# New orders, engine choices and PSUM banks for a four-layer attention kernel

## The chip, the core and the metric

The kernel runs on one core of one Trainium2 chip. The metric is the device time of one execution in microseconds (us), as the median of several runs. The engines are PE (TensorE; its weight loads are listed apart, as PEld), DVE (VectorE), ACT (ScalarE), POOL (GpSimd) and SP (SyncE, which only issues DMAs here).

## The reference

Four layers with residual sums act on x of 2048 tokens by 512 features, in bf16. Layers 1 and 3 are linear attention with 32 heads of 16, layers 2 and 4 softmax attention in a window of 256 keys:

```python
x = x + _A_ref(_layernorm(x), A_wqkv, A_wo)   # phi(q) (phi(k)^T v) / (phi(q) sum phi(k)), then @ wo
x = x + _B_ref(_layernorm(x), B_wqkv, B_wo)   # softmax over keys with 0 <= i - j < 256, then @ wo
x = x + _A_ref(_layernorm(x), A_wqkv, A_wo)
x = x + _B_ref(_layernorm(x), B_wqkv, B_wo)
# phi(t) = where(t > 0, t + 1, exp(t)) + 1e-6
```

## The kernel before, in words

The tokens are cut into 16 tiles of 128. x (`xres`), all weights and the keys and values of four tiles stay in SBUF. PSUM is used as eight banks of 128 x 512 fp32 (one bank is a tile of the plan).

The program is written as a graph of 2559 operations (`Graph.add`, class `Op`). An operation is one thing that one engine does: a group of matmuls, an eviction from PSUM, a mask, a DMA. It knows what it reads and writes and which PSUM tiles it uses. The names that the prediction and the experiments use are these:

- `norm` (the line numbers are the profile's): statistics (L374, DVE), their aggregate (L375, DVE), variance plus epsilon (L379, POOL; L377 on DVE for a few), the power -1/2 (L380, POOL), the subtraction and scaling (L381, DVE), and a transpose by DMA (L389, SP) or for a few tiles by PE (L395) with an eviction (L402).
- `tok` (L420) and `feat` (L434): the projections on PE, token-major and feature-major. L501 to L524 are the sums over keys of layer 1, L480 and L477 those of layer 3 and their normalizers.
- `phi`: the exponential (L444, ACT), minimum (L447, DVE), and the maximum (L451, DVE, or L446 on ACT and L449 on DVE).
- Plain evictions (L407): `bqe` of queries and `bve` of values of the softmax layers, `ve` of the values of layer 3, `ge`, `Me` and `sc` in the passages between layers. `bke` (L627 on ACT, L628 on DVE) evicts keys into a spread layout. Each of these may be ACT's or DVE's.
- `s` (L676, L712, L745, L792): scores of one tile of keys, in parts; `ex` (L686, L721, L754, L801): their exponentials on ACT; `mk` and `md` (L694, L726): causal masks on DVE; `mf`: the masks of the far keys, on POOL (L772) or DVE (L773). `pv` (L822): products with the values; `rcp` and `div` (L834, L835); `oT`: the transposed output; `bout` (L420): the output projection; `res` (L604): the residual sum on DVE. `outp` (L942): the store of one tile of the result, from SP or POOL; the very last tile is stored in two halves (L878, after L877).
- `fill`: seven matmuls on zeros that PE runs at the start, beside nine before them.

Layer 1 computes all keys first; then a passage with PE's L501 to L579 follows; layer 2 then goes tile by tile, interleaved with the norms and keys of layer 3. After a second passage (layer 3's queries, sums and normalizers) comes layer 4, with the output projection of layer 3 interleaved tile by tile.

What sets the order: one table, `TABLE`, a compressed string. `place(g)` (L92) unpacks it. It holds, for 2559 operations, the overall order (two bytes each), the engine of each operation (one byte each), and the bank of each of 1005 PSUM tiles (one byte each). Each engine issues its operations in that order, and no other. A PSUM tile waits for all users of the tile that held its bank before. For a few pairs `place` adds a wait: a long POOL operation (`LONG`) waits for the short DVE operation (`SHORT`) that stands last ahead of it in the order. `synchronise` then turns dependences into semaphore waits.

```python
order = [ops[raw[2 * k] + 256 * raw[2 * k + 1]] for k in range(n)]
o.eng = ("PE", "ACT", "DVE", "POOL", "SP")[raw[2 * n + o.i]]
x.banks = [raw[3 * n + k]]
```

The planner's keys and costs in `PAR` don't count here, since the table overrides them.

Of the kernel before, what the change touches and what calls it, by code (L numbers as in the profile page):

```python
# [235 lines left out]
class Plan:  # L236
# [718 lines left out]
    r"c-qZZ1GH_+j;*AUO4YS(+qP}nwr$(CZQHhO+h*^z&%Lkz@5lf8{~o>0SxP0TnVDHN_6n(#3ZYPu0>vt{(khG!tBeY#;;UdPxccG}D67J&gzBTqtRkpSE~5J8",  # L955
    r"5~(cegG;Qksun7VilmaNY^tS-tg@?Cs*n2YqNp6IwMwQYsGKUfimLi5QE62hl|uDX(NtR%N~Ke|RXdeZEmn<GdevXmRuk0{HA!Vqb<_a0O)XUeRbACyrBahs",
    r"V>L)^R~^(cHAU4^JJeJaL)BLuRT{NZEmtvBF_lrRP@U9ZwM)fPomF&oOYK&%RYR3Y4N<q%3Ds5IQA1TX6;}mT2I8o@s=Lag;;Cuso@$~}tCMP&y050IH|msX",
    r"sv4-_YKA(kR;rn5l{%y5s#)r+TCEDIE=r(>daH`7HEN#9t0F*8wMPX~7J8`>s)SmrMk)ur)hP8&1%ml1BJ5SURA4BhvcMd*PmNZIV1b&g_N(_QE38usRV4VJ",
    r"&Zz_HqlygYRdrPi8o&khKqZDKkOYduLv>L_g>2AFtyh=SBb84bRF72<$PQ0bP$&VHRSpOSC84>>2~X7+6&yaPr0`jdQ)5*rIHbO)WY7?j!&emzzNxAzI$Tj9",
    r"pftpQ{OXyC2?}CC1(ge&8n1Fg5S0Q7sXUMp@<J#`1^J+`Dg$L9HGEfPRT>xvjUXhHgE$aW6;S0N9aMnvPyi}H5!D!KLu_aYwP2A-3sqEps0c+>JE#FQVS}ou",  # L960
    r"+Cv?v3-zF!st+BY2^?0Pp@wP$9iauZg;vlKHmWYr3|hkx)d`wIcX+Ojs;{mGOn|O%OihI2YLlw0UZ_d1SzT2x)k4^!CPO8)2(GCq&<&=-3D~L@!*$gYrol;=",
    r"4mZ>$SOV45W>^X{;1mEXgPCwsAuNZvumUvnf_bnKN~&2<Ud@Lsa2RT-*{}e%!V#DQ+n_g`hNG|@*1{{*57xnP*a0_TJ?w;4&<A$GYUm5MU=5rBf{?fYUaPZk",
    r"8%kqMbqxB$J=h4Lkl_K8!E+EAOR3OsAI`%wD2o>$47`BdP!9J%SO|l6VIMq)aBv6q!(NDm2Ounlhqn+8W8*srj~Ah|ii4NnJw(8`_y{h;6?g&%p*&uNhfo0{",
    r";sAII*B~)g#DQ=gli~$D1eLH3Cc%qX8RO$qsEY}3EY`ytFb)&q2e=NYaXfy6PmmVlVS4xs8K6FXfi!pttKdtxjIUq<W`rx49wT7}oQSXCDrSPnI0=(sReS>(",
    r"aWY21sE8O16Ja&X3=OdXCdcU52&>~YOo5GY3bw^eI2CJPI&6<AaUQ0^`B)R%p~mY-xB#0XV`glQ9WV<Te1OgHD+p%AhiEYyeurt82Opus>G%zrU`GsuG4Te@",
    r"z|MFR17i!U47acoDy#y4*)cEH#vGUrYhg>wiTSY=7Qh%-6&7O`j0;OKH_pUrFbiAb608onFbEdJpx6eN;c_g5!EiR-#+7&ngJWTg2SqRhuE3($74Kp<j1Q}D",
    r"J$A<guo@TPMob86um^6yemDr$;yN4*n{gp-#i39Pi{lX3f)VvFh@>}R34Dp$@HLji?N|zT;46%*zhV?!O@G7cdMEC}{`ehh=mYo^qv`=zQ$NROx*!b1Cs+ug",
    r">t`54_ryUMQzz1e;RVjtz3>gr(SxxFJkYgtQK+qZV`BXnhu~cOP$$ttu@8R4gZK%D;URpahhtwH4xjNb?nb5O;#=H<BcP7HkMD3Ve!)4ITG!R@5%dvEtM?=7",
    r"4_Hs9(T{a<y$@sQCtB;2I<_W#4@Y1e{Zt3iDfCE8r=RJ}dY&GIjdW6-MaR{naSX=OS@nE<6tnA8`WQCW@pTTJUN_Olae>aDbLxe<jb5ZP>iW8^&ZHaY6PQc4",
    r"(<iZmey#)SY`UTDsDtQaI=61GgX&J2bsil|8{J$7*Ligd-C2jwqVwq<x}`3nd+9aW>QmTLC(urx#>KjiK7(s@Kix&I(;;<h-BtJ1p>!*K7B}i{`W%MVn{`p$",  # L970
    r"T^G~+^(Nh0Z`H;10G&{8(<Ssky<L~o`SliEN)OV@byGc97tkwoY28dO(Pi{Xy+Ie$d-YPiUw_nv^)g*nf71K(NC=}x>QV4nht;DYoIa>u=&_KL4(ntTUXOu7",
    r"x|}|w*XsznyiQIP^bkEt57ia*OI=C7(!+EL8m)KellrwzNn>;?N=2u1YdWG+(@uRrpVnz;mmaRu(pZf&Lch^OZD_TAt9R?8dX*lhHMOPj`k3CM-{}eZtp29c",
    r"(Q&P4qFzrY^dx;oZ=mlw5N)LNbWR5*pp2A(GEop>`l5r;CNlIvhoGP&)Q;Zk%+#KOQ*QdI&+87<k@C_7ZE3Q06q54L6n#-=qwF+QU()%h6HU{h=&~+A)Abb{",
    r"nsU%pU64vs7|KasC@htwuT+R4Q$FfOW$2pjPTwdO6{o^fj!M#Xy_tGY5!yl}XaH@cqSTp+(LgFiUFbWNr$MB+D-EFvG?cc{4PB9L>S0ugYEU>jK(}-h3QxCn",
    r"RJx;kQv`}eS*Q;kr0BGr`cg!iK!<3Co<uWs49ZH8C??gUi8Poh(=1(!Vo_BBj!nC1IK`noRGW~i&=}G@g6a_QI2uWNX)GP3$<&W_P+b~D_2?M&r=2vOM$=tg",
    r"pL)`9x~CgZFN#aMs5;%(4XGNPq$zZYrqXG;N{4A0ouGI$ovzanvh4U81?50Imx6J8x<MD|3^k(56r3AV0y;~VC?TDrCUk{D@p-yQO(`^Apk{Q7!f-ea$+u}9",
    r"-J$S2pO_a=1b#%(I4m1pNYObbhu~bih=gPCVrovgc?K<^7POyc(qn2#`{)VHqL>_upHd=<&57w5wdFXxl<razT1K;}9p9%p^qgOC5WYtzxIG8vlN^y>aw3kz",
    r"uQ&<E<>wTcU-Jt}%**K%zoZrPfTD0zF2pM-9v9(N6rW$wYD&t5IUncc1iXe4@@vY^YbhB&q>H?cPICdy!=?BVC+9MJhA;CKF3knG92e!Qe3mP4F}}vdxjc8{",
# [190 lines left out]
```

## Time and profile before

| | |
|---|---|
| median of 3 runs | 412.56 us (412.19 to 414.08) |
| span of the profiled execution, first to last instruction | 410.8 us |
| granted TensorE clock | 1.000 |
| DMA, mean | 91 GB/s |
| operations by the table: PE, ACT, DVE, POOL, SP | 866, 447, 806, 212, 228 |

The profiled execution has no other time than its span; the median of the runs is 1.8 us above it, for what lies around the first and the last instruction. The profile page gives busy times by engine, the chain of work that ended last (followed back from the last instruction, at each step to what released it), and groups of instructions by line. In a row such as "L694 DVE TENSOR_TENSOR pb<-pb,tri 128x512 ...", the tile written stands left of the arrow, and those read right of it.

### The profile page before, as it was taken

What the parts mean: (1) busy time and instruction counts of PE and PEld (TensorE: products, weight loads), DVE (VectorE), ACT (ScalarE), POOL (GpSimd) and SP (SyncE); (2) the same over time, 40 slices, a digit from 0 to 9 for tenths busy, and PEclk for the clock granted to TensorE, in tenths of its full rate; (3) what the DMA queues carried; (4) which work ended last, traced back from release to release, by engine and by line L of the source; (5) the groups of instructions that cost most, each with busy time, mean ns of one, the idle gap of its engine ahead of it and who ended that gap; (6) DMA issues with size and microseconds to landing.
All of it is one profiled execution on the core that took longest, in us unless ns stands there. A gap on an engine that the chain in (4) does not pass through costs nothing.

```text
span 410.8 us, 17540 instructions
## 1 busy us (share of the span) xinstructions
PE 386.9 (94%) x7668; PEld 260.3 (63%) x7742; DVE 344.5 (84%) x807; ACT 352.8 (86%) x448; POOL 122.4 (30%) x216
## 2 busy tenths in 40 slices
PE   7999999999999999999999999999999988999896
PEld 3654676766575576566567777586757755566674
DVE  6997799989998899888887789997899688857585
ACT  4654659998999999999998357999999999999993
POOL 4576653111252331320503203303113304303020
PEclk9999999999999999999999999999999999999999
DMA  7495114443243435353222100344314821561751
GB/s 249 101 217 144 49 34 115 120 70 90 56 106 74 119 77 107 81 119 82 68 41 57 27 2 2 105 109 81 102 44 122 122 66 41 120 127 56 168 107 42
DMA packets 66596, 37.19 MB, mean 91 GB/s; under 512 B 47640, under 2 KB 61848, under 8 KB 66520
## 3 DMA queue, kind: packets, MB, share of 16 engines
q1 hardware_dynamic: 66032, 34.75, 37.0%
q8 instruction: 61, 1.00, 1.1%
q0 software_dynamic: 480, 1.31, 1.0%
q14 instruction: 15, 0.12, 0.1%
q10 hardware_dynamic: 8, 0.00, 0.0%
HBM read 6.29 MB, written 2.10 MB: 20 GB/s over the span
## 4 chain that ended last, share of the span: by engine, by line
PE 51%; ACT 34%; DVE 9%; DMA 3%; issue 2%; SPq 1%; POOL 1%
ACT pb L686 20%; PE ps L420 18%; PE ps L434 10%; PE ps L822 10%; PE ps L676 5%; ACT pb L801 5%; ACT vp L686 4%; PE ps L501 3%; ACT tE L444 2%; DMA wA<-in_A_wqkv_dram 2%; DMA xT<-xn 1%; DVE xres L604 1%; DVE stats L374 1%; ACT pb L721 1%; PE ps L477 1%
## 5 line engine op out<-in xcount | busy, mean ns | idle before, releaser
L686 ACT ACTIVATE pb<-ps 128x1024 bf16<-128x1024 f32 (+2 forms) x216 | 198.9, 1020 | 5.2 <-PE ps L676 3.9
L822 PEld LDWEIGHTS ps<-vB,pb 128*128 128x128 bf16 x2560 | 77.7, 96 | 12.3 <-DVE pb L694 3.6
L822 PE MATMUL ps<-vB,pb 128*128 128x34 bf16 x2560 | 83.5, 177 | 0.6 <-POOL pb L772 0.3
L434 PE MATMUL ps<-xT,wBp 128*128 128x128 bf16 x1024 | 69.0, 219 | 1.7 <-ACT tE L444 0.6
L434 PEld LDWEIGHTS ps<-xT,wBp 128*128 128x128 bf16 x1024 | 58.5, 98 | 13.7 <-issue 4.4
L379 POOL TENSOR_SCALAR ve<-mv 128x1 f32<-128x1 f32 x63 | 16.7, 265 | 154.7 <-DVE mv L375 152.7
L444 ACT ACTIVATE tE<-ps 128x512 bf16<-128x512 f32 x64 | 38.6, 612 | 27.1 <-PE ps L420 11.2
L772 POOL TENSOR_SCALAR_AFFINE_SELECT pb<-pb 128x1024 bf16<-128x1024 bf16 x30 | 34.4, 1146 | 71.4 <-DVE pb L694 23.8
L676 PE MATMUL ps<-XQ,kB 32*128 32x256 bf16 (+3 forms) x992 | 48.0, 267 | 3.3 <-ACT pb L754 0.7
L604 DVE TENSOR_TENSOR xres<-ps,xres 128x512 bf16<-128x512 f32 x63 | 43.0, 684 | 6.7 <-PE ps L420 6.3
L420 PE MATMUL ps<-wA,XQ 128*128 128x512 bf16 x174 | 45.6, 379 | 2.2 <-issue 0.6
L374 DVE BATCH_NORM_STATS2 stats<-xres 128x6 f32<-128x512 bf16 x64 | 43.5, 685 | 2.8 <-DMA xres<-in_A_x_dram 2.2
L694 DVE TENSOR_TENSOR pb<-pb,tri 128x512 bf16<-128x512 bf16 (+1 forms) x108 | 41.5, 396 | 3.3 <-ACT pb L686 3.1
L801 ACT ACTIVATE pb<-ps 128x1024 bf16<-128x1024 f32 x42 | 41.4, 1059 | 1.1 <-PE ps L792 0.9
L380 POOL TENSOR_TENSOR rs<-ve,negh 128x1 f32<-128x1 f32 x64 | 37.8, 591 | 8.3 <-DVE ve L377 3.0
L434 PE MATMUL ps<-XQ,wA 128*128 128x128 bf16 x512 | 35.4, 219 | 0.3 <-DMA wA<-in_A_wqkv_dram 0.3
L434 PEld LDWEIGHTS ps<-XQ,wA 128*128 128x128 bf16 x512 | 30.7, 98 | 7.3 <-DMA wA<-in_A_wqkv_dram 0.8
L420 PE MATMUL ps<-wBv,xT 128*128 128x512 bf16 x110 | 31.4, 380 | 2.6 <-issue 1.0
L676 PEld LDWEIGHTS ps<-XQ,kB 32*128 32x128 bf16 x992 | 15.0, 92 | 29.5 <-ACT pb L686 7.5
L420 PE MATMUL ps<-M,XQ 128*128 128x512 bf16 x113 | 30.7, 380 | 2.3 <-ACT vp L686 0.4
L420 PE MATMUL ps<-wBo,oT 128*128 128x512 bf16 x105 | 28.8, 380 | 2.8 <-issue 1.0
L686 ACT ACTIVATE vp<-ps 128x1024 bf16<-128x1024 f32 (+2 forms) x32 | 26.7, 928 | 1.5 <-PE ps L676 1.5
(126 smaller groups left out, 551.6 us busy)
## 6 DMA issues: line engine op xcount, KB each, us to landing
vB<-vS SPq DMA_DIRECT2D x64, 136.0 KB, 2.7
kB<-vp SPq DMA_DIRECT2D x60, 128.0 KB, 2.3
wA<-in_A_wqkv_dram SPq DMA_DIRECT2D x3, 512.0 KB, 5.5
out_dram<-xres POOLq DMA_DIRECT2D x10, 128.0 KB, 2.8
xres<-in_A_x_dram SPq DMA_DIRECT2D x2, 512.0 KB, 5.1
pb<-in_B_wqkv_dram SPq DMA_DIRECT2D x1, 1024.0 KB, 5.8
xres<-in_A_x_dram SPq DMA_DIRECT2D x3, 256.0 KB, 5.5
out_dram<-xres SPq DMA_DIRECT2D x5, 128.0 KB, 2.7
```

Of the source, the lines that this page charges most:

```text
L374: self.on("DVE", "stats", lambda e: e.bn_stats(K.stats[:, t, :], x()), key, dve(512), rd=rd, wr=[("stats", t)], **held)
L380: self.pow = self.on("POOL", "pow", lambda e: e.tensor_tensor(K.rs[:, t, :], K.ve[:, t, :], K.negh[:], ALU.pow), key + 0.03, (640, 690), r ...
L420: m = e.matmul(K.ps(ps), lhs(c), rhs(c), start=c == 0 and not whole, stop=c == 3)
L434: m = e.matmul(K.ps(ps)[:, f * P:(f + 1) * P], w(c, f), xT(c), start=c == 0, stop=c == 3)
L444: self.on("ACT", "E", lambda e: e.activation(K.tE[:, s, :], K.ps(ps), ACT.Exp, bias=0.0), key, act(512), wr=[("tE", s)], ps=[ps])
L604: self.on("DVE", "res", lambda e: e.tensor_tensor(K.xres[:, t, :], K.ps(po), K.xres[:, t, :], ALU.add), key, dve(512), rd=[("xres", t)], w ...
L676: m = e.matmul(K.ps(ps[gq])[:, ns * i:ns * i + ns], K.kB[rows, j % 4, 2 * f + b, :, :], K.XQ[rows, f, q:q + ns], start=True, stop=True, ti ...
L686: return e.activation(out(2 * h, 2, ns), i, ACT.Exp, bias=0.0, scale=0.25)
L694: return e.tensor_tensor(x, x, K.tri[:, 0, sh:64].unsqueeze(1).unsqueeze(1).to_broadcast([P, 4, n, 64 - sh]), ALU.mult)
L772: return e.affine_select(out=x, in_=x, compare_op=ALU.is_ge, fill=0.0, base=-2, pattern=[[0, 16], [-2, 64]], channel_multiplier=1)
L801: return e.activation(far(h), i, ACT.Exp, bias=0.0, scale=0.25)
L822: m = e.matmul(K.ps(ps)[:, 34 * u:34 * u + 34], K.P((b // 2) % rp)[:, gq, f, o:o + P], K.vB[:, (b // 2) % 4, b % 2, r, :], start=i == 0, s ...
```

## The change

Only the table is replaced. The code, the operations, their tiles and their sizes stay.

```diff
 TABLE = (
-    r"c-qZZ1GH_+j;*AUO4YS(+qP}nwr$(CZQHhO+h*^z&%Lkz@5lf8{~o>0SxP0TnVDHN_6n(#3ZYPu0>vt{(khG!tBeY#;;UdPxccG}D67J&gzBTqtRkpSE~5J8",
...
+    r"c-qZb1F&pK($31ttgL#rZQHhO+qP}nwr$(CZQK0&^nEk`?9R^Yo7sqst&TpYPFCW}FSE1njRpt}VIV9Z#D@eB0)jy}2oB*PAtVBV%#a1LLN@s1BEU!Y&3$%X",
...
 )
```

Unpacked, the two tables compare like this. 2404 of the 2559 places of the overall order hold another operation. 51 operations have another engine:

| operation | from, to | how many |
|---|---|---|
| evictions (`bqe` 4, `bke` 3, `ve` 3, `bve` 2, `ge`, `Me`, `sc`, `Te` 1 each) | ACT to DVE | 16 |
| evictions (`bqe` 2, `ve` 2, `bke`, `bve`, `ge`, `sc`, `oTe` 1 each) | DVE to ACT | 9 |
| masks of far keys `mf` | DVE to POOL | 12 |
| masks of far keys `mf` | POOL to DVE | 8 |
| stores `outp` | POOL to SP, SP to POOL | 3, 3 |

(`Te` and `oTe` are the evictions of transposes that PE made.) The counts become PE 866, ACT 440, DVE 809, POOL 216, SP 228. 599 of the 1005 PSUM tiles have another bank. Of the operations that keep their engine, the largest set that also keeps its mutual order is 656 of 866 on PE, 368 of 431 on ACT, 492 of 785 on DVE, 134 of 201 on POOL and 141 of 225 on SP.

106 lines of the change are left out of this document (53 added, 53 removed).

## The prediction

> **What bounds the kernel now.** I start at the top of the page: the span, the engines' busy shares, and the chain of work that ended last.
>
> ```profile
> span 410.8 us, 17540 instructions
> PE 386.9 (94%) x7668; PEld 260.3 (63%) x7742; DVE 344.5 (84%) x807; ACT 352.8 (86%) x448; POOL 122.4 (30%) x216
> ...
> PE 51%; ACT 34%; DVE 9%; DMA 3%; issue 2%; SPq 1%; POOL 1%
> ```
>
> Three engines are over 80% busy and the chain changes hands between PE and ACT. So the average decides nothing, and I cut the span where the chain changes hands. The columns are busy us (and instructions) of PE, its weight loads, DVE, ACT and POOL, then the granted clock.
>
> ```profile
> core 0: us, PE busy (x) PEld busy (x) DVE busy (x) ACT busy (x) POOL busy (x), PEclk, DMA share, GB/s
> 0.00:60.00 60.00, 56.80 (x562) 33.72 (x571) 50.74 (x129) 31.98 (x55) 35.85 (x77) 1.00 0.50 133
> 60.00:103.00 43.00, 41.19 (x809) 29.48 (x818) 40.21 (x92) 40.17 (x48) 9.92 (x19) 1.00 0.43 99
> 103.00:148.00 45.00, 41.76 (x905) 26.70 (x907) 40.77 (x96) 44.56 (x53) 14.43 (x24) 1.00 0.37 86
> 148.00:225.00 77.00, 74.80 (x1574) 49.57 (x1588) 65.12 (x154) 72.98 (x89) 21.17 (x32) 1.00 0.37 81
> 225.00:259.00 34.00, 33.34 (x518) 24.69 (x525) 29.15 (x70) 20.56 (x38) 7.62 (x15) 1.00 0.09 22
> 259.00:293.00 34.00, 33.15 (x673) 23.26 (x678) 30.24 (x69) 34.00 (x40) 8.22 (x13) 1.00 0.38 89
> 293.00:324.00 31.00, 29.57 (x679) 20.83 (x680) 26.93 (x63) 30.52 (x35) 8.04 (x13) 1.00 0.48 95
> 324.00:395.00 71.00, 64.46 (x1708) 44.20 (x1716) 52.07 (x122) 69.62 (x82) 14.00 (x22) 1.00 0.44 97
> 395.00:411.00 16.00, 11.79 (x270) 7.84 (x270) 9.29 (x23) 8.40 (x16) 3.21 (x4) 0.99 0.31 78
> ```
>
> Layer 1 (0 to 60) and the passage from layer 3 to layer 4 (225 to 259) leave ACT idle: 28.0 and 13.4 us. There PE sets the pace. Where the two attention layers run (60 to 225, 259 to 395), ACT is 93 to 100% busy, and PE 91 to 98%. The chain, cut to three of these stretches (103 to 148, 259 to 293, 324 to 395), says who is last:
>
> ```profile
> by line: ACT pb L686 45.0%; ACT pb L801 12.2%; PE ps L434 9.0%; ACT tE L444 6.1%; PE ps L420 5.8%; PE ps L822 5.6%; PE ps L676 4.1%; DVE pb L694 2.2%; issue 1.6%; DVE vp L451 1.5%; DVE xres L604 1.4%; DVE stats L374 1.3%; ACT vS L407 1.2%;
> by line: ACT pb L686 51.0%; ACT pb L801 16.3%; ACT pb L721 11.1%; ACT vp L686 8.1%; ACT tE L444 5.8%; ACT vp L627 3.5%; issue 3.2%; PE ps L676 1.1%
> by line: ACT pb L686 54.3%; ACT vp L686 20.8%; ACT pb L801 7.9%; ACT pb L754 4.3%; PE ps L822 3.5%; PE ps L420 2.5%; PE ps L676 1.6%; ACT vp L754 1.4%; PE ps L745 1.3%; issue 0.9%; PE ps L792 0.7%; ACT XQ L407 0.7%; PE ps L434 0.2%
> ```
>
> These are ACT's: about two thirds, 96% and 89%. An instruction that leaves ACT there is worth its place in ACT's queue; one that leaves ACT elsewhere is worth little, because PE is next to it.
>
> **The change, part by part.** Nothing is added or removed; the decoded table moves work between engines and reorders queues.
>
> *Work off ACT.* 16 evictions go from ACT to DVE and 9 from DVE to ACT, so ACT loses a net 7 of 447. By the time at which each runs now: net 1 before 60; 1 in 60 to 148 (out at 79, 84 and 146, in at 95); 2 in 148 to 225; 1 in 225 to 259; 1 in 259 to 293 (out at 270.8 and 273.4, in at 270.7); none in 293 to 324; 1 in 324 to 395 (out at 368.0). What one is worth is the step from its start to that of the next on a full ACT, not its duration. ACT's rows, in time order:
>
> ```profile
> 270.80 0.90 ACT L627 ACTIVATE vp<-ps 128x512 bf16<-128x512 f32 x1
> 271.57 1.94 ACT L686 ACTIVATE pb<-ps 128x1024 bf16<-128x1024 f32 x2
> 273.39 0.75 ACT L627 ACTIVATE vp<-ps 128x512 bf16<-128x512 f32 x1
> 274.01 1.02 ACT L686 ACTIVATE pb<-ps 128x1024 bf16<-128x1024 f32 x1
> ...
> 367.99 0.63 ACT L407 ACTIVATE XQ<-ps 128x512 bf16<-128x512 f32 x1
> 368.49 1.05 ACT L686 ACTIVATE vp<-ps 128x1024 bf16<-128x1024 f32 x1
> ```
>
> So a key eviction (L627) takes 0.77 and 0.62 us of the queue, a plain one 0.50. In 259 to 293: 0.77 + 0.62 out, 0.50 in, **-0.9 us**. In 324 to 395: **-0.5**. In 60 to 148: three plain ones out (1.5), one key eviction in (0.7, between those two), 0.8; but ACT has 2.8 us idle before 103, so part of it is lost there, and I take **-0.5**, with bounds 0 and -0.8. In 148 to 225: a key eviction and two plain ones out, two plain ones in, by the same steps -0.7; the chain there is mostly PE's, and I take 0. Before 60, in 225 to 259 and in 293 to 324 I take 0: PE's 56.8 of 60, 33.3 of 34 and 29.6 of 31 us are the cover, and none of them loses work.
>
> The Trainium skill says, in "Perfetto Trace Analysis", section "Identifying the Most-Contended Engine", that matmul busy time doesn't show how full TensorE is, and that the share of the weight loads does. By that share (49.6 of 77 us, 64%) PE has room in 148 to 225, and the sum would be 0.7 us lower; the trace alone doesn't settle it, since the chain there does run through PE.
>
> *Work onto DVE.* Each eviction costs DVE about 0.69 us. Masks of the far keys (L772 on POOL, L773 on DVE) also change sides: 12 to POOL, 8 to DVE. By the rows' times and 0.69 and 0.68 us each, DVE has 4.1 us more work by 330 us (6 evictions net; 6 masks in, 6 out), and 2.1 more at the end (7 evictions net; 8 masks in, 12 out). It has idle time for that: 2.8, 4.2, 11.9, 4.9, 3.8 and 4.1 us in the stretches from 60 to 324. I take nothing; the bounds are 0 and +4.1, if DVE becomes last.
>
> *Masks.* One of POOL's masks stands on the chain now, beside its twin on DVE; here are the rows of the chain, of DVE and of POOL, then the same pair of engines at 179, and the group of undisturbed masks on DVE:
>
> ```profile
> 89.04 1.16 POOL pb L772
> ...
> 89.52 1.20 DVE L773 TENSOR_TENSOR pb<-pb,tri 128x1024 bf16<-128x1024 bf16 x1
> ...
> 89.04 1.15 POOL L772 TENSOR_SCALAR_AFFINE_SELECT pb<-pb 128x1024 bf16<-128x1024 bf16 x1 [2.10 <-DVE pb L694]
> ...
> 179.95 1.24 DVE L773 TENSOR_TENSOR pb<-pb,tri 128x1024 bf16<-128x1024 bf16 x1
> ...
> 179.51 1.15 POOL L772 TENSOR_SCALAR_AFFINE_SELECT pb<-pb 128x1024 bf16<-128x1024 bf16 x1 [0.72 <-DVE xn L381]
> ...
> L773 DVE TENSOR_TENSOR vp<-vp,tri 128x1024 bf16<-128x1024 bf16 x3 | 2.0, 677 | 0.0
> ```
>
> A DVE mask begun beside a POOL mask took 1.20 and 1.24 us, one alone 0.68: DVE stood until POOL was through. In the new table both masks of the pair at 89 are DVE's (2 x 0.68, one cast that ran at 88.91 put behind them and one at 83.8 and one statistics ahead: done between 90.0 and 90.7, against 90.72) and both of the pair at 179 are POOL's. The first is on the path: **-0.4** (bounds 0 and -0.7). The two collisions that go are 0.52 + 0.56 = 1.1 us of DVE; DVE is on the path 9% of the time but feeds both others, so I take half: **-0.5** (bounds 0 and -1.1). The masks that go to POOL, and so take 0.47 us longer, end 3.6 us or more before the first product that reads them begins (the nearest is the one at 314.5, read at 318.7). The ones that come to DVE at 89, 130, 221 and 395 had 0.5 to 1.7 us. So the longer masks are covered.
>
> *Reordered queues.* Apart from these, PE keeps 656 of its 866 operations in their old mutual order, ACT 368 of the 431 that it keeps, DVE only 492 of 785, POOL 134 of 201, SP 141 of 225. PE's and ACT's orders in layer 4 are almost the old ones; DVE's is new, and 599 of 1005 PSUM tiles have another bank. One wait that this could touch is on the chain between 316 and 326:
>
> ```profile
> 316.10 0.69 DVE xres L604
> ...
> 317.98 0.41 DVE xn L381
> ...
> 318.42 4.92 DMA xT<-xn
> 323.34 0.14 issue
> 323.47 0.61 PE ps L434 x8
> ```
>
> A transpose waits for DVE's subtraction, and PE for the transpose. In the new DVE list the statistics of this tile (L375) no longer stand behind that residual sum, but the subtraction has one more cast ahead of it: between -0.6 (the transpose starts when the statistics allow) and +0.7. On SP, the output transpose of tile 4 now goes out ahead of it. I take 0.
>
> *The tail.* These are rows of the chain's end, and of the output stores:
>
> ```profile
> 401.26 0.81 PE ps L420 x3
> ...
> 405.14 0.81 PE ps L420 x3
> ...
> 407.65 0.42 DVE xres L877
> ...
> out_dram<-xres POOLq DMA_DIRECT2D x10, 128.0 KB, 2.8
> ...
> out_dram<-xres SPq DMA_DIRECT2D x5, 128.0 KB, 2.7
> ```
>
> The projection of tile 13 (401.26) moves behind the last value products, where PE now waits for DVE, and that of tile 14 (405.14) behind tile 15's. PE reaches the last products up to 0.8 us earlier and ends with 0.8 us more behind them; the last sum is then a whole one (0.69) in place of a half (0.42), and its store goes out on POOL, the last three of POOL's in a row. Between -0.8 and +0.8; I take 0.
>
> **The sum**: -0.9 - 0.5 - 0.5 - 0.4 - 0.5 = -2.8 us. The span of the profiled execution, 410.8, becomes 408.0; the median of the runs, 412.56, is 1.8 above that span, and with the same 1.8 the time is **409.8 us**.
>
> **The rivals.** *More goes than ACT's load.* ACT's idle time in 60 to 225 and 259 to 395 is 9.2 us (2.8 + 0.4 + 4.0 + 0.5 + 1.4, rounded up). It is spent in short waits for PE, and the new lists may close them. A third of it, and the 0.7 us of 148 to 225, give 409.8 - 3.1 - 0.7 = 406.0. For it: all queues and banks were free to move. Against: PE and ACT keep their order where these waits are. *PE takes it all.* PE is busy 33.2 of 34 us where ACT is 34.0 of 34; if PE is really full there, only 324 to 395 (64.5 of 71) gives its 0.5, and the mask its 0.4: 411.7, not to be told from no change. *DVE becomes last.* This one is slower. From 60 to 324 DVE does 4.1 us more; it goes through one queue in order, and subtractions, residual sums and bank-freeing casts all wait behind it, with the transposes and so PE behind those. If its idle time there stays where it is, in waits for PE and ACT, nothing absorbs the 4.1: 412.56 - 0.5 + 4.1 = 416.2. It decides once fewer than 4.1 of DVE's 31.6 idle us lie ahead of an instruction that is late; at half of it the time is 414.1. *POOL's masks stop DVE.* Twelve masks newly on POOL, each stopping a DVE instruction by 0.52 as at 89.52, would be 6.2 us: with the sum, 416.0. Of the 33 masks that are on POOL now only a few do so, which speaks against it. The Trainium skill says the same of the mechanism in "SBUF — State Buffer", section "SBUF: two separate sides": the two engines share a pair of ports, and whoever starts first keeps the other out for the whole instruction. The rows at 89 and 179 agree.
>
> **How the numbers follow.** The forecast (407.8 to 410.5 with its own bounds) gets 0.42; more goes, 0.16; PE takes it all, 0.24; DVE last, 0.13; masks stop DVE, 0.05. About 0.5%, 2.1 us, is what a measurement of this kernel can tell from no change, so faster means below 410.5, slower above 414.6: 0.58 faster, 0.24 same, 0.18 slower. The range goes from a little under the first rival, 405.5, to DVE's half case, 414.1.
>
> **What would show it.** In the changed profile: ACT with 440 evictions and exponentials and about 4 us less busy time, no DVE mask of 1.2 us at 89 and 179, and the stretch from the first to the last exponential of layer 4 about 1.4 us shorter. DVE last would show as a DVE share of the chain well above 9%, more PE and ACT waits that DVE ends, and later transposes. The prediction is wrong if layer 1 or the passage at 225 to 259 changes its length by over 1 us, for which I have no term.

## The result and the profile after

The changed kernel takes 411.58 us (median, 410.26 to 413.44) against 412.82 us for the kernel before in the runs beside it. The ratio of their times is 0.9966, with a 95% interval of 0.9949 to 0.9982: 1.4 us faster, with an interval of 0.7 to 2.1 (the medians differ by 1.2). I had forecast 2.8 us and 409.8. The profiled execution after belongs to a run of 412.81 us, 1.2 above its median, so its span isn't the measure; its stretches are.

The head of the page after: the span, the busy times, and the chain that ended last.

```profile
span 411.0 us, 17617 instructions
...
PE 395.9 (96%) x7742; PEld 262.0 (64%) x7742; DVE 345.8 (84%) x810; ACT 350.1 (85%) x441; POOL 130.7 (32%) x220
...
PE 73%; ACT 14%; DVE 9%; DMA 2%; issue 1%; SPq 0%; POOLq 0%; POOL 0%
```

ACT is 2.7 us less busy, not 4, and its share of the chain fell from 34 to 14%. PE looks 9 us busier, though it does the same work. That is mostly the record: before shows 7668 matmuls for 7742 weight loads, after all 7742. Here is PE with the old table and a full record, from the page of e5 (below) and its window from 148 to 225:

```profile
PE 395.1 (96%) x7742; PEld 260.2 (63%) x7742; DVE 343.2 (84%) x807; ACT 346.0 (84%) x448; POOL 122.2 (30%) x216
```

```profile
148.00:225.00 77.00, 76.98 (x1592) 49.73 (x1585) 65.03 (x155) 70.75 (x89) 20.68 (x32) 1.00 0.40 82
```

So PE was at 96% before too, and what I quoted for 148 to 225 (74.80 of 77) was short by some 2 us of records. The chain's shares depend on the record as well: with DVE's cut (below) and every matmul recorded, PE and ACT have 62 and 25% with the old table (e7), 69 and 23% with the new (e8). So the fall from 34 to 14% isn't the table's alone. The same stretches after, columns as in the prediction's table:

```profile
0.00:60.00 60.00, 58.03 (x567) 34.24 (x567) 52.20 (x130) 31.09 (x53) 37.27 (x79) 1.00 0.48 137
60.00:103.00 43.00, 42.23 (x825) 29.79 (x822) 40.58 (x93) 40.15 (x48) 8.35 (x16) 1.00 0.42 93
103.00:148.00 45.00, 42.52 (x932) 27.10 (x928) 41.09 (x95) 44.08 (x52) 14.73 (x22) 1.00 0.45 90
148.00:225.00 77.00, 76.99 (x1566) 49.57 (x1563) 65.20 (x155) 71.94 (x87) 21.94 (x34) 1.00 0.37 78
225.00:259.00 34.00, 33.95 (x532) 24.97 (x530) 29.50 (x71) 21.58 (x39) 8.29 (x15) 1.00 0.13 25
259.00:293.00 34.00, 33.28 (x679) 23.22 (x678) 29.95 (x70) 33.00 (x39) 6.87 (x11) 1.00 0.36 90
293.00:324.00 31.00, 30.83 (x720) 21.55 (x718) 27.34 (x63) 30.59 (x36) 8.64 (x12) 1.00 0.40 89
324.00:395.00 71.00, 66.41 (x1687) 43.83 (x1685) 50.99 (x119) 69.59 (x81) 21.42 (x26) 1.00 0.46 96
```

In 259 to 293, ACT went from 34.00 to 33.00 of 34: the instructions that left did leave. Their time became ACT's own waiting: in this stretch it now stands 0.8 us for scores of L676 and 0.2 for those of L792, and before it stood for none. Over the whole span its waits for scores of L676 doubled; here are the rows (us in total, times, longest), the first of before, the second of after:

```profile
ACT pb L686 <- PE ps L676: 3.9, 8, 1.0
```

```profile
ACT pb L686 <- PE ps L676: 7.6, 17, 0.8
```

And the chain after for 259 to 293, where before ACT had 96%:

```profile
by line: PE ps L434 33.7%; PE ps L420 25.2%; PE ps L822 15.2%; PE ps L676 13.2%; ACT pb L686 5.7%; ACT pb L801 2.7%; PE ps L792 2.0%; PE ps L563 1.2%; PE ps L712 1.0%; issue 0.4%
```

ACT has handed the last place to PE there (in e7, the old table with a full record, ACT still has three quarters of it), and the stretch isn't shorter. To see where time came and went, I cut all runs at marks in the work, not at clock times: the end of the last sum of L524 in layer 1, then the last exponential of a tile (layer.tile), then the end of the span. Lengths in us, worked out from the traces:

```
                 A           B           C            D            E            F             tail
       sums   to 2 tile 1  to tile 12  to 4 tile 0  to tile 4   to tile 5   to tile 13   to end
before 42.2    50.0        108.8        70.2         43.5         12.0        65.7         18.5
after  42.8    48.8        109.3        69.6         44.0         11.2        66.1         19.1
e4     41.9    48.5        109.0        69.6         43.9         11.2        65.7         18.5
e1     41.9    51.1        110.5        71.3         43.8         11.3        65.8         18.4
e12    41.8    50.0        109.0        71.3         43.5         11.3        65.8         18.4
e11    41.9    52.0        114.3        74.4         44.6         11.7        66.8         18.9
e14    41.8    48.5        109.8        71.0         44.6         11.4        66.8         18.9
e13    41.8    48.5        109.3        69.6         44.7         11.2        66.7         20.7
e17    42.5    48.7        109.3        69.6         43.2         11.2        65.7         18.4
e18    41.8    48.7        111.2        70.2         43.2         11.2        65.8         18.4
```

By these marks the gain is in A (the passage after layer 1 and the ramp of layer 2) and C (the passage to layer 4), and B and D got longer. But these marks don't part the same work. The new order has PE run four more matmuls of L501 ahead of the mark in layer 1 (about 0.9 us), and eight of L434 behind the last scores of tile 1 (about 0.45 us) that the old one runs ahead of them. PE is busy 49.75 us of A in e5 (old table, all matmuls recorded) and 48.52 after. So A has 1.2 us less work of PE in it, about as much as it got shorter, and it can't be read as a saving. Whether that work is the reason isn't shown either: e2 (below) takes ten matmuls out of A and leaves its length as it was. At five marks PE has done the same operations with both tables: the end of the last L501 in layer 1, and the last scores of tiles 2.12, 4.4, 4.5 and 4.13. With the exponentials of these scores as marks, the lengths are (e7 and e8 are the old and the new table with the same cut on DVE):

```
         start to    to 2      to 4     to 4     to 4      tail
         last L501   tile 12   tile 4   tile 5   tile 13   to end
before   43.9        157.0     113.7    12.0     65.7      18.5
after    43.7        157.2     113.6    11.2     66.1      19.1
e4       42.8        156.6     113.5    11.2     65.7      18.5
e7       43.2        156.6     113.5    12.1     66.0      18.4
e8       43.0        156.9     113.4    11.2     66.0      18.9
```

From the last L501 to tile 4 of layer 4 nothing is gained clear of chance. What differs is layer 1 (43.2 to 44.3 in the eight profiled executions with the old order, 42.6 to 43.7 in the twelve with the new, with a cut or none; 43.7 and 42.9 on the mean), the one tile from 4.4 to 4.5, and the tail, which costs 0.5. Why layer 1 is shorter isn't shown.

**The first exponential of layer 2.** These are rows of before (ACT and PE, in time), then those of its waits for the weight loads of L579 and L712; then the same instructions after.

```profile
56.12 0.60 ACT L444 ACTIVATE tE<-ps 128x512 bf16<-128x512 f32 x1 [0.76 <-PE ps L434]
56.61 1.70 ACT L624 ACTIVATE kB<-ps,par 128x512 bf16<-128x512 f32 x2
...
58.37 0.40 PE L579 MATMUL ps<-rec,spread 32*128 32x128 bf16 x16
...
62.89 2.85 ACT L721 ACTIVATE pb<-ps 128x1024 bf16<-128x1024 f32 x3 [0.51 <-PE ps L712]
```

```profile
PEld ps L579 <- ACT kB L624: 0.6, 1, 0.6
PEld ps L712 <- ACT vS L407: 0.4, 1, 0.4
```

```profile
58.34 0.83 ACT L624 ACTIVATE kB<-ps,par 128x512 bf16<-128x512 f32 x1 [0.30 <-PE ps L434]
...
59.50 0.84 ACT L624 ACTIVATE kB<-ps,par 128x512 bf16<-128x512 f32 x1
...
58.23 0.40 PE L579 MATMUL ps<-rec,spread 32*128 32x128 bf16 x16
...
61.92 1.02 ACT L721 ACTIVATE pb<-ps 128x1024 bf16<-128x1024 f32 x1
```

Before, two evictions of keys (L624) on ACT held a bank for which PE's L579 waited, and one of values the bank for the first scores (L712). The first exponential of layer 2 began at 62.89, 19.0 us after the last L501. After, neither wait is there, with the evictions of keys behind L579, and the first exponential comes at 61.92, 18.2 us after the last L501. That is a matter of order and banks alone, as these evictions are ACT's in both tables, and I had no term for it. It isn't all gain: L579 comes 14.5 us after the last L501 with both tables, and four matmuls of L420 (about 0.9 us) that the old order runs ahead of these scores now stand behind them.

**The tail** ends with a whole residual sum and a store on POOL; here are DVE's and POOL's last rows of after, then DVE's and SP's of e4:

```profile
407.31 0.69 DVE L604 TENSOR_TENSOR xres<-ps,xres 128x512 bf16<-128x512 f32 x1
...
408.29 0.54 POOL L942 DMA_DIRECT2D out_dram<-xres  x1 [1.93 <-DVE xres L604]
```

```profile
404.98 0.88 DVE L882 TENSOR_TENSOR xres<-ps,xres 128x256 bf16<-128x256 f32 x2 [0.18 <-PE ps L876]
...
405.43 0.81 SPq L883 DMA_DIRECT2D out_dram<-xres  x2
```

### The profile page after: what moved, and what is told of

Same layout as the page of the kernel before. It is cut to its first block, busy times and chain, and to the rows that moved or that the text cites. A ratio compares the mean times of both kernels' runs of the same rounds, so it can differ in the third digit from the quotient of the medians.

```text
span 411.0 us, 17617 instructions
## 1 busy us (share of the span) xinstructions
PE 395.9 (96%) x7742; PEld 262.0 (64%) x7742; DVE 345.8 (84%) x810; ACT 350.1 (85%) x441; POOL 130.7 (32%) x220
## 4 chain that ended last, share of the span: by engine, by line
PE 73%; ACT 14%; DVE 9%; DMA 2%; issue 1%; SPq 0%; POOLq 0%; POOL 0%
PE ps L420 24%; PE ps L434 17%; PE ps L822 15%; ACT pb L686 8%; PE ps L676 7%; PE ps L501 3%; ACT vp L686 3%; DVE XQ L591 2%; ACT pb L801 2%; PE ps L792 1%; DMA oT<-o 1%; DMA kB<-vp 1%; DVE xres L604 1%; PE ps L1082 1%; PE ps L477 1%
## 5 line engine op out<-in xcount | busy, mean ns | idle before, releaser
L434 PE MATMUL ps<-xT,wBp 128*128 128x128 bf16 x1024 | 69.0, 220 | 0.6 <-ACT pb L686 0.4
L434 PEld LDWEIGHTS ps<-xT,wBp 128*128 128x128 bf16 x1024 | 59.0, 98 | 12.1 <-issue 4.4
L772 POOL TENSOR_SCALAR_AFFINE_SELECT pb<-pb 128x1024 bf16<-128x1024 bf16 x32 | 37.4, 1167 | 64.0 <-DVE pb L694 31.7
L604 DVE TENSOR_TENSOR xres<-ps,xres 128x512 bf16<-128x512 f32 x63 | 42.9, 684 | 10.6 <-PE ps L420 10.2
L676 PE MATMUL ps<-XQ,kB 32*128 32x256 bf16 (+3 forms) x992 | 48.2, 268 | 3.3 <-DVE vp L628 0.9
L420 PE MATMUL ps<-wA,XQ 128*128 128x512 bf16 x192 | 49.7, 380 | 0.7 <-DVE vp L451 0.5
L374 DVE BATCH_NORM_STATS2 stats<-xres 128x6 f32<-128x512 bf16 x64 | 43.7, 683 | 2.4 <-DMA xres<-in_A_x_dram 1.8
L380 POOL TENSOR_TENSOR rs<-ve,negh 128x1 f32<-128x1 f32 x64 | 39.2, 613 | 8.3 <-DVE ve L377 3.0
L420 PE MATMUL ps<-wBv,xT 128*128 128x512 bf16 x128 | 35.3, 382 | 0.9 <-ACT pb L801 0.5
L434 PE MATMUL ps<-XQ,wA 128*128 128x128 bf16 x512 | 35.2, 219 | 0.1
L420 PE MATMUL ps<-wBo,oT 128*128 128x512 bf16 x124 | 33.4, 381 | 1.6 <-ACT pb L801 0.7
L434 PEld LDWEIGHTS ps<-XQ,wA 128*128 128x128 bf16 x512 | 30.6, 98 | 6.2 <-ACT pb L686 0.8
L420 PE MATMUL ps<-M,XQ 128*128 128x512 bf16 x128 | 33.6, 381 | 0.9 <-ACT vp L686 0.5
L676 PEld LDWEIGHTS ps<-XQ,kB 32*128 32x128 bf16 x992 | 15.0, 92 | 27.3 <-ACT pb L686 9.4
L835 DVE TENSOR_TENSOR o<-ps,rc 128x256 bf16<-128x256 f32 x64 | 26.8, 420 | 1.3
```

Source lines behind the costliest of these rows:

```text
L374: self.on("DVE", "stats", lambda e: e.bn_stats(K.stats[:, t, :], x()), key, dve(512), rd=rd, wr=[("stats", t)], **held)
L380: self.pow = self.on("POOL", "pow", lambda e: e.tensor_tensor(K.rs[:, t, :], K.ve[:, t, :], K.negh[:], ALU.pow), key + 0.03, (640, 690), r ...
L420: m = e.matmul(K.ps(ps), lhs(c), rhs(c), start=c == 0 and not whole, stop=c == 3)
L434: m = e.matmul(K.ps(ps)[:, f * P:(f + 1) * P], w(c, f), xT(c), start=c == 0, stop=c == 3)
L604: self.on("DVE", "res", lambda e: e.tensor_tensor(K.xres[:, t, :], K.ps(po), K.xres[:, t, :], ALU.add), key, dve(512), rd=[("xres", t)], w ...
L676: m = e.matmul(K.ps(ps[gq])[:, ns * i:ns * i + ns], K.kB[rows, j % 4, 2 * f + b, :, :], K.XQ[rows, f, q:q + ns], start=True, stop=True, ti ...
```

## The experiments

Kernels with an edit in `place` have their later lines 2 to 9 numbers further on (e4's L882 is L877). All ratios are to the kernel before, run beside them; us are worked out with 412.5.

```
                                         ratio   95% interval       us to before
after                                    0.9966  0.9949 to 0.9982      -1.4
e1  evictions' engines alone             1.0095  1.0078 to 1.0111      +3.9
e12 masks' engines alone                 1.0029  1.0010 to 1.0049      +1.2
e11 orders and banks alone               1.0335  1.0308 to 1.0361     +13.8
e14 changed, masks' engines undone       1.0086  1.0067 to 1.0105      +3.5
e13 changed, four evictions undone       1.0001  0.9986 to 1.0017       0.0
                                         old table                  new table
PE 13.8 us less          e2  0.9984 (0.9970 to 0.9999)   e3  0.9922 (0.9901 to 0.9942)
ACT 7 us less            e5  0.9994 (0.9976 to 1.0013)   e6  0.9979 (0.9961 to 0.9997)
DVE 13 us less           e7  0.9988 (0.9974 to 1.0001)   e8  0.9962 (0.9948 to 0.9975)
PE and ACT less          e9  0.9953 (0.9935 to 0.9971)   e10 0.9909 (0.9879 to 0.9939)
all three less           e15 0.9942 (0.9923 to 0.9960)   e16 0.9875 (0.9857 to 0.9893)
e4  tail's order mended                  0.9955  0.9940 to 0.9970      -1.9
e17 and three exchanges                  0.9949  0.9931 to 0.9966      -2.1
e18 and five more                        0.9989  0.9967 to 1.0010      -0.5
```

The theories stand as each expectation names them. From e5 on, Theory 1 is the prediction's: in each stretch the work of the full engine sets the time. In e7 and e8 it says only that DVE isn't last. Theory B (at first Theory 2): the fixed orders tie the engines together, and chains of waits through the queues set it.

### Parts of the table

Each part is put in or taken out where `place` unpacks the table, like this (e13, on the changed kernel; 1725 and 1780 are key evictions, 1777 and 2339 of queries):

```diff
-    raw = zlib.decompress(b85decode("".join(TABLE)))
+    raw = bytearray(zlib.decompress(b85decode("".join(TABLE))))
     n = len(ops)
+    for i, e in {1725: 1, 1777: 2, 1780: 1, 2339: 1}.items():
+        raw[2 * n + i] = e
```

**e1**: the old table with the 25 evictions on their new engines.

> The old orders, banks and masks; only the 25 evictions are on the engines that the new table gives them (16 from ACT to DVE, 9 from DVE to ACT). Theory 1, PE is full wherever the attention layers run and ACT only looks last: ACT's time turns into waits for PE, and the time stays within 0.6 us of the kernel before. Theory 2, ACT's relief is real and something else in the new table gives it back: 1.9 us less than before, the sum of the three ACT terms of the prediction (0.9 + 0.5 + 0.5).

It is 3.9 us slower: A +1.1, B +1.7, C +1.1. Neither theory had that. At their old places the moves cost nearly what DVE's rows say (7 net evictions of 0.69 us are 4.8), DVE's share of the chain rises from 9 to 14%, and ACT's relief doesn't show.

**e12**: the old table with the 20 masks on their new engines.

> The kernel before, with only the 20 far masks on their new engines, at their old places in the order. By the prediction's terms for the masks (0.4 for the one at 89, 0.5 for two collisions of DVE with POOL): 0.9 us faster, 411.2 to 411.9. Rival: 12 masks moved to POOL stop DVE or end late where the old order did not leave room for them, 1 to 4 us slower (413 to 416).

1.2 us slower; in the segments C is 71.3 for 70.2. The rival's number holds, though I haven't followed which mask makes C longer. A is 50.0 as before. The two masks at 89 and the collisions, for which I had counted 0.9, are worth nothing at the old places.

**e11**: the new orders and banks with all old engines (45 operations, and six stores that had changed between POOL and SP).

> The changed kernel's orders and banks with the engines of before (the 25 evictions and 20 far masks go back to their old engines at their new places). The evictions' engines alone, in the old table, cost 3.6 us. If the gain is the orders' and the engines only load DVE: 0.5 to 3 us faster than the changed kernel (408 to 411). If orders and engines were chosen for each other (an eviction stands in DVE's list where DVE has room): 1 to 5 us slower than it (412.5 to 416.5). By the prediction's terms (1.9 us for ACT's relief, 0.9 for the masks): 2.8 us slower, with no difference to before.

13.8 us slower, far outside all that I expected: A to D and F are all longer. One of its waits: a key eviction of layer 2 that the new table has on ACT at this place is DVE's again (98.99, then a subtraction at 99.60), and PE's projection waits for DVE, and ACT for PE:

```profile
98.99 0.71 DVE L630 CAST vp<-ps 128x512 bf16<-128x512 f32 x1
99.60 0.39 DVE L383 TENSOR_SCALAR xn<-xres,mv,rs 128x512 bf16<-128x512 bf16 x1
...
100.06 0.81 PE L422 MATMUL ps<-wA,XQ 128*128 128x512 bf16 x3 [1.36 <-DVE xn L383]
...
100.90 0.60 ACT L446 ACTIVATE tE<-ps 128x512 bf16<-128x512 f32 x1 [1.39 <-PE ps L422]
```

PE stood 1.36 us and ACT 1.39 behind one eviction of 0.71 us, which stood behind other casts in DVE's queue. By the plan PE needs the bank that this eviction frees, and not the subtraction that the profile names. The three parts alone cost 3.9, 1.2 and 13.8; together they gain 1.4. Nothing here adds up: an order is an order for given engines.

**e14**: the changed kernel with the masks' engines undone.

> The changed kernel with the 20 far masks back on their engines of before, at their new places; with the 25 evictions back as well the time was 14 us longer. If the 14 are the evictions' (they free PSUM banks for which PE waits): 0.5 to 2 us slower than the changed kernel, 412 to 414. If the masks carry half or more: 5 us or more, above 416.

3.5 us slower than before, so 5.0 slower than the changed kernel, at the edge of the second case. By subtraction from e11, as far as the parts add up, the evictions (and the six stores) carry about 10 us of the 15 and the masks 5. A is 48.5 with the masks undone too, so the mask at 89 has no part in A's gain.

**e13**: the changed kernel with the four evictions behind my two ACT terms undone.

> The changed kernel with the four evictions of my terms for 259 to 293 and 324 to 395 (two key evictions and two of queries; net three on ACT) back on their engines of before, at their new places. By the prediction's step (an instruction less on ACT is worth its place in the queue: 0.9 and 0.5 us): 1.4 us slower than the changed kernel. Theory B (load is worth nothing; a wait in the order is): these four stand where ACT and DVE were planned to have room, so 0 if the places are covered either way, and up to 3 us slower where a score waits for the bank that an eviction frees.

Against the changed kernel 1.4 us (0.9966 to 1.0001; the intervals don't overlap, and leave 0.5 to 2.4), as the prediction's step had it. In the segments, D is 44.7 against 43.8 to 44.0 and F 66.7 against 65.7 to 66.1. (The 20.7 of its tail is of the profiled execution, whose granted clock was 0.994.) ACT's rows of after and then ACT's and PE's of e13, at the first of the four:

```profile
268.63 1.94 ACT L801 ACTIVATE pb<-ps 128x1024 bf16<-128x1024 f32 x2 [0.15 <-PE ps L792]
270.45 0.60 ACT L407 ACTIVATE XQ<-ps 128x512 bf16<-128x512 f32 x1
271.21 1.94 ACT L686 ACTIVATE pb<-ps 128x1024 bf16<-128x1024 f32 x2 [0.16 <-PE ps L676]
```

```profile
267.28 1.94 ACT L803 ACTIVATE pb<-ps 128x1024 bf16<-128x1024 f32 x2 [0.15 <-PE ps L794]
269.11 0.75 ACT L629 ACTIVATE vp<-ps 128x512 bf16<-128x512 f32 x1
270.37 1.02 ACT L688 ACTIVATE pb<-ps 128x1024 bf16<-128x1024 f32 x1 [0.51 <-PE ps L678]
271.29 0.74 ACT L629 ACTIVATE vp<-ps 128x512 bf16<-128x512 f32 x1
...
269.92 0.40 PE L678 MATMUL ps<-XQ,kB 32*128 32x256 bf16 x8 [0.43 <-ACT vp L629]
```

The eviction takes its place (0.75 for 0.60), and more: the scores need the bank that it frees, PE waits 0.43 us for it, and ACT then 0.51 for PE.

### Less work, the same order

Three cuts of work, alone and together: half the matmuls of the first of two groups in each output projection, half the columns of 20 far exponentials, half the row in all statistics.

```diff
-                for c in (2 * h, 2 * h + 1):
+                for c in ((0,) if h == 0 and name in ("aout", "bout") else (2 * h, 2 * h + 1)):
...
-            def ex(e, h=h):
+            def ex(e, h=h, thin=h and (self.rp > 3 or j > 2)):
                 i = pair(ps[2 * h:2 * h + 2], [[128, 4], [64, 2], [1, 64]])
+                if thin:
...
-        self.on("DVE", "stats", lambda e: e.bn_stats(K.stats[:, t, :], x()), ...
+        self.on("DVE", "stats", lambda e: e.bn_stats(K.stats[:, t, :], x()[:, 0:256]), ...
```

**e2 and e3**: PE's cut, in the old table and the new.

> The kernel before, with the second of the four matmuls of every output projection (layers 1 to 4, 64 in all) left out, so its result lacks a quarter of those products; PE has 64 x 0.216 = 13.8 us less work. Theory 1: PE is last over most of the span, so 5 to 9 us go, until ACT is last. Theory 2: ACT is last in 103 to 148, 259 to 293 and 324 to 395; only what lies outside these counts, 2 to 5 us.

> The changed kernel with the same 64 matmuls left out (its result lacks a quarter of the output projections' products). To be set against the kernel before with the same cut. Theory 1: with PE out of the way the seven evictions off ACT get their worth, so it is 2 to 3.5 us under that kernel, clearly more than the 1.2 us between the two whole kernels. Theory 2: the relief was there already, and the difference stays at about 1.2 us.

0.7 and 1.8 us (0.9966 to 0.9922) of 13.8; both ranges of e2 are missed. (The 13.8 goes by the step from matmul to matmul; in the pages, which both lack records, PE's busy time fell by 8.5.) A row of 96% doesn't mean that PE's work sets the time. e3 is 2.6 us under e2, as its Theory 1 had it, but with an interval of 1.5 to 3.6 that isn't clear of the 1.4 between the whole kernels.

**e5 and e6**: ACT's cut.

> Kernel before, with 20 of the 46 exponentials of the far keys (L801: 11 in layer 2, 9 in layer 4) half as wide, 512 columns in place of 1024, so that one head group in four keeps old values in its far keys; by the rows 1.06 against 0.59 us, ACT loses about 9.3 us of work and no operation. Theory 1 (that of the prediction: ACT's queue is last in most of the attention layers, an instruction less is worth its place): 6 to 8 us faster than before, 404.5 to 406.5. Theory 2 (the three engines are tied to each other by fixed orders, and one engine's relief turns into its own waiting): 0.5 to 2.5 us faster, 410 to 412, and ACT's idle time in layers 2 and 4 grows by 7 us or more.

> The same 20 narrower exponentials in the changed kernel, ACT 9.3 us less. Theory 1: 6 to 8 us under the changed kernel (403.5 to 405.5). Theory 2: 0.5 to 2.5 us under it (409 to 411). Theory 3 (the new orders moved the limit from ACT to PE: the cut of 13.8 us on PE gave 0.9 us with the old table and about 2.4 with the new): under 0.8 us here and over 3 us in the old table.

0.2 us with the old table, its interval from 1.0 faster to 0.5 slower, where Theory 1 had 6 to 8; in the new 0.5 slower than the changed kernel, within the two intervals no difference. Theory 1 falls here, and Theory 3 with it (the old table should have given over 3). Theory 2's 0.5 to 2.5 isn't reached in either. Its other sign came: ACT's idle time in 60 to 225 and 259 to 395 grew from 9.2 to 15.9 us in e5, by all that ACT lost. By the profile that was 6.8 us (352.8 to 346.0), not the 9.3 that I had worked out.

**e7 and e8**: DVE's cut (12.8 us by the profile in e7).

> Kernel before, with all 64 statistics (L374) over 256 of the 512 columns, so that mean and variance are those of half a row; by 0.69 us each, about 64 x 0.27 = 17 us less work on DVE, 9 of it from 60 us on. Theory 1 (DVE is third and not last): within 0.8 us of before. Theory 2 (tied engines; DVE hands on what PE and ACT wait for; 7 net evictions more on DVE at their old places cost 3.6 us): 2 to 5 us faster, 408 to 411.

> The same narrower statistics in the changed kernel. Theory 1: within 0.8 us of the changed kernel. Theory 2: 1.5 to 4 us faster than it (407.5 to 410). If DVE's new order has already removed the waits that its old order made, the gain is under half of the old table's.

0.5 and 0.2 us: Theory 1's numbers hold, and Theory 2's 2 to 5 and 1.5 to 4 don't. DVE's load isn't last either, though by e1 and e11 it matters what stands where in its queue.

**e9 and e10**: PE's and ACT's cuts together.

> Both cuts with the old table: 64 matmuls of the output projections left out (13.8 us of PE) and 20 far exponentials at half width (9.3 us of ACT; one head group keeps old far keys). Alone they gave 0.7 and 0.25 us. Theory A (PE and ACT are both full in the attention layers, so one's relief shows only the other): far more than the sum, 5 to 9 us faster than before, 403 to 407. Theory B (what binds is chains of waits through the fixed orders, DVE and the transposes, and not work): about the sum, 0.5 to 2.5 us, 410 to 411.5.

> Both cuts in the changed kernel. Alone they gave about 2 to 3 us (PE) and about 0 (ACT) under the changed kernel. Theory A: 6 to 10 us under it, 401 to 405. Theory B: 2 to 3.5 us, 408 to 409.5. Either way a difference to the old table with both cuts of more than 1.2 us would say that the new order is better than the work on PE and ACT lets show.

1.9 us faster with the old table, 2.4 (0.9966 to 0.9909) with the new: Theory A, that the two engines hide each other's relief, falls; Theory B's numbers hold. With both cuts the new table is 1.8 us under the old one, without them 1.4; the intervals (0.9935 to 0.9971 and 0.9879 to 0.9939) touch, so the cuts don't tell the two tables further apart.

**e15 and e16**: all three.

> The old table with all three cuts: 13.8 us less on PE, 9.3 on ACT, about 17 on DVE (half-row statistics, outer products of the output projection left out, 20 narrow far exponentials). Both cuts of PE and ACT gave 1.9 us, DVE alone 0.5. Theory A' (DVE is the third full engine, and only all three together free the pipeline): 5 us or more faster, under 407.5. Theory B: 2 to 4 us, 408.5 to 410.5, though each engine has at least 9 us less to do.

> The changed kernel with all three cuts. PE's cut alone gave 2 to 3 us under the changed kernel, and with ACT's the same. Theory A': 6 us or more under it, below 405.5. Theory B: 2.5 to 4.5 us, 407 to 409.

The page of e15:

```profile
span 406.6 us, 17415 instructions
...
PE 374.7 (92%) x7606; PEld 254.7 (63%) x7679; DVE 330.6 (81%) x807; ACT 346.0 (85%) x448; POOL 122.5 (30%) x216
```

With 13.8 us less on PE by the step (12.2 by the pages), 6.8 on ACT and 13.9 on DVE the time falls by 2.4 us (0.9942), and in the new table by 3.8 against the changed kernel (0.9966 to 0.9875). Theory A' falls, and Theory B's numbers hold. A in the old table is 49.9 or 50.0 in all six profiled executions of it with a cut or none, and 48.3 to 48.8 in all eleven with the new orders other than e11 (from the last L501, 48.2 and 47.4 to 47.9): the order sets it, whatever the load.

### Order alone

**e4**: the last 37 places of the changed table in another order (tile 13's and 14's projections back ahead of the last tile's), the stores of tiles 13 and 14 on SP, one bank changed.

> The changed kernel, with its last 37 places put in another order: tile 14's projection goes in the gap that PE has while tile 15's last heads are divided, and tile 15's sum is the last one again; the stores of tiles 13 and 14 go out from SP. If the tail gives back what the layers gain, the span ends 0.5 to 0.8 us earlier than the changed kernel's, 1.7 to 2.0 us under the kernel before; the last sum on DVE ends about 2.7 us before the span does, not 3.0. If the tail is hidden or the gain is elsewhere, the time is the changed kernel's, 1.2 us under the kernel before.

0.9955: 0.5 us under the changed kernel, though the intervals overlap; the tail is 18.5 against 19.1 and ends with DVE and SP as in the rows above.

**e17**: e4, and three pairs of neighbours exchanged.

```diff
     order = [ops[raw[2 * k] + 256 * raw[2 * k + 1]] for k in range(n)]
+    for x, y in ((743, 748), (1761, 1886), (2255, 2250)):
+        order.insert(order.index(ops[y]), order.pop(order.index(ops[x])))
```

> The changed kernel with the mended tail of e4 and three pairs of neighbours exchanged in queues of SP and DVE, nothing else: the second key copy of tile 7 (layer 2) ahead of a value copy on SP, where an eviction and then PE and ACT waited 0.46 us at 122; the transpose of the first output of layer 4 ahead of another transpose on SP, where PE waited 0.4 us at 278 and ACT 0.46 at 280; a mask of layer 4's tile 9 ahead of a reciprocal on DVE, where PE waited 0.3 us at 360. No engine has less to do. Theory B (waits made by the order bind): each wait closes, 0.8 to 1.3 us under e4, 409.1 to 409.7. Theory 1 (work of the full engine binds): no difference to e4, within 0.3 us.

0.9949, 0.2 us under e4 and within its interval. That is below Theory B's 0.8 to 1.3, and the number that Theory 1 gave. But nothing was done to any load, and segment by segment the three exchanges had different fates. For the second exchange, here are e4's SP, PE and ACT rows and then e17's:

```profile
273.06 1.19 SPq L394 DMA_TRANSPOSE xT<-xn  x1
274.29 1.27 SPq L394 DMA_TRANSPOSE oT<-o  x1
...
278.68 1.02 PE L425 MATMUL ps<-wBo,oT 128*128 128x512 bf16 x4 [0.56 <-DMA oT<-o]
...
280.09 1.02 ACT L691 ACTIVATE pb<-ps 128x1024 bf16<-128x1024 f32 x1 [0.46 <-PE ps L681]
```

```profile
273.74 1.20 SPq L396 DMA_TRANSPOSE oT<-o  x1
274.98 1.27 SPq L396 DMA_TRANSPOSE xT<-xn  x1
...
278.96 1.03 PE L427 MATMUL ps<-wBo,oT 128*128 128x512 bf16 x4
...
280.49 1.98 ACT L693 ACTIVATE pb<-ps 128x1024 bf16<-128x1024 f32 x2
```

PE's 0.56 and ACT's 0.46 us are gone, and D is 43.2 in both e17 and e18, against 43.9 in e4: this wait was worth its length, and D is now shorter than the old table's 43.5. The first exchange only moved the wait: e4's PE waited for the eviction, e17's products then stood, by the profile's name, for a mask:

```profile
122.12 0.40 PE L681 MATMUL ps<-XQ,kB 32*128 32x256 bf16 x8 [0.58 <-DVE vp L633]
```

```profile
121.82 1.35 PE L829 MATMUL ps<-vB,pb 128*128 128x34 bf16 x48 [0.98 <-DVE pb L701]
```

So tile 4 of layer 2 came 0.3 us later. The profile names DVE's mask, but that had ended at 121.46. Here are e17's mask and the value copy, now third on SP:

```profile
121.05 0.41 DVE L701 TENSOR_TENSOR pb<-pb,tri 128x512 bf16<-128x512 bf16 x1
...
118.10 0.60 SPq L662 DMA_DIRECT2D vB<-vS  x1
```

By the trace's DMA records this copy landed at 121.73, and the products began at 121.82. In e4 the third copy, of keys, was issued at 117.45 and landed at 121.31. In both, the copy that goes third lands 3.6 to 3.9 us after its issue (the two before it 2.0 to 2.5), and what reads it is late. The third exchange gained 0.4 us by tile 10 of layer 4 and lost it again by tile 11.

**e18**: five scores ahead of the projection before them on PE.

> The same, and five more exchanges on PE: a group of scores ahead of a projection of layer 2 or 3 that stood right before it while ACT waited (at 79, 169, 179, 217 and 221; ACT's waits there 0.73, 0.22, 0.50, 0.69, 0.50 us). Each score begins up to 0.43 us earlier, and PE stands up to 0.3 us for the bank that the last exponential frees. If those waits of ACT set the time: another 0.8 to 1.6 us under e17. If PE's own queue sets it there: none, or up to 0.8 us slower.

0.9989, 1.6 us slower than e17, which is more than the 0.8 that I had allowed; B is 2.0 longer. ACT's waits for scores were not the last thing there; what came late instead, I haven't followed.

## Why the prediction was right or wrong

The direction was right; the size was twice what came, and the measured terms are not the forecast ones. By the prediction's own line (faster means below 410.5) 411.58 is even no change; 17 runs of each kernel tell smaller differences apart than the 0.5% that it had taken. Its range for the forecast, 407.8 to 410.5, doesn't follow from its terms: with their upper bounds the time is 411.2, with those of the queues and the tail 412.7. And in its list the net moves off ACT of two stretches are exchanged (2 in 60 to 148, 1 in 148 to 225); the terms use the right ones.

- **The failed step** is the part "Reordered queues", where 599 new banks and a new DVE order were taken at 0, while each engine move was priced at its old place. e11 shows the orders without their engines at +13.8 us, and the engines at their new places at -15. The forecast was a sum of small terms around a sum of two large ones that I had not seen.
- **ACT's relief (-0.9, -0.5).** At the new places the moves are worth 1.4 us (e13), as the step from row to row had it, though a wait for a bank that the step doesn't have is part of it. But the new order without them is longer than the old: D 44.7 against 43.5, F 66.7 against 65.7. The relief pays that back: D +0.4, F between 0 and +0.4. In 60 to 148 the -0.5 isn't there (from the last L501 to 2.12, 157.0 before and 156.6 to 157.2 after, in e4 and in e17). Layer 4 from its first to its last exponential, which should be about 1.4 shorter, takes 144.0 us before, 144.2 after and 143.9 in e4.
- **"An instruction that leaves ACT there is worth its place"** holds for four instructions on which a bank hangs, and not for work as such: 6.8 us less on ACT gave 0.2 (e5).
- **Masks (-0.4, -0.5).** The rows came as forecast. Here are DVE's pair at 89 and the group of its masks, after:

```profile
88.33 1.28 DVE L773 TENSOR_TENSOR pb<-pb,tri 128x1024 bf16<-128x1024 bf16 x2
```

```profile
L773 DVE TENSOR_TENSOR pb<-pb,tri 128x1024 bf16<-128x1024 bf16 x18 | 12.7, 709 | 0.0
```

  Both are done at 89.61, 1.1 us before the old 90.72, and a mask takes 709 ns on the mean (766 before). The time did not follow: e12 is 1.2 slower, and A is the same with or without. What stood behind the mask must have been late for another reason, which no row here shows.
- **Zeros.** Two places at which the prediction said that it had no term did change. Layer 1 to its last L501 is 0.7 us shorter on the mean, half of the measured gain. Between the last exponential of layer 2 and the first of layer 4 there are 32.7 us for 34.3, over the 1 us that the prediction named as a sign against it; but more of the work stands ahead of it, and from 2.12 to 4.4 nothing is left of that. The DMA wait at 318 comes in three of the eight executions with the old order (landings of 4.9 to 5.5 us; E 12.0 to 12.4, else 11.1 to 11.4) and in none of the eleven with the new without e11 (11.1 to 11.4): the change may have taken 0.3 to 0.4 us there on the mean. The tail, 0 with bounds of 0.8, cost 0.5.
- **Rivals.** "PE takes it all" named 411.7, and 411.58 came, but not by its mechanism: PE less loaded by 13.8 us gives 0.7 (e2). "DVE last" was priced at 4.1 for the work on DVE; e1 comes near that case at 3.9; in the changed kernel DVE's share of the chain is 9% as before, and the case doesn't come.
- **By the Trainium skill's reading of PE.** The sentence drawn from the Trainium skill ("Perfetto Trace Analysis", "Identifying the Most-Contended Engine") gave PE room in 148 to 225 and 0.7 us more. Those 0.7 didn't come, and PE's busy time there was 76.98 of 77 with a full record; but e2's cut shortened B by only 0.9 us, so the full row didn't set the stretch's length either. The same section says to optimise the engine with the highest occupancy first, and to judge TensorE by its weight loads or by what it computes against its peak. By the weight loads (63%) that is ACT with the old table (86%, DVE 84%), and 6.8 us less on it gave 0.2.

## What to carry to other kernels

Where a hand-made order runs over several queues that are all nearly full, price a move at its new place and with what waits for it, not by the busy time that it takes or leaves; three parts that cost 3.9, 1.2 and 13.8 us alone can gain 1.4 together. When two orders are compared piece by piece, take marks ahead of which the fullest engine has done the same operations; else work that moved past a mark looks like a gain, as A did here. To know whether load or order binds, cut work from the full engine without touching the order: if little of the cut comes back (0.7 of 13.8 us here), look for single waits at exchanged neighbours, like the 0.56 us of e17. And closing a wait is worth its length only if nothing queued behind takes its place, which one of three exchanges managed.

## What was not expected of the hardware

A profile can lack matmul records (74 of 7742 in the profile before), which makes PE look 8 to 10 us less busy: compare the count of matmuls with that of weight loads before a window's PE time is read as room. Layer 1 up to its last L501, with the start's loads, varies by up to 1.2 us between executions of one order, nearly as much as the change brings.

What stays open: which of the 599 changed banks matter, why layer 1 is shorter with the new table, and what of the 1.4 us lies elsewhere. The best version tried, e17 (0.9949), and e4 (0.9955) beat the kernel before; their intervals overlap that of the changed kernel.
